# Another order and another spread over the engines for a chunk-selected attention with an ELU feed-forward block

## Chip, cores and metric

The kernel runs on one core of one Trainium2 chip. The metric is the device time of one execution in microseconds (us). The core has TensorE (PE, with its weight loads as PEld), VectorE (DVE), ScalarE (ACT), GpSimd (POOL) and SyncE (SP), and 16 DMA engines that are fed by queues. Each engine works off its own instructions in program order.

## The reference, cut to what matters

```python
batch, n_heads, seq, head_dim = (4, 8, 768, 64)      # q, k, v in float32
n_tokens, d_model, d_ff = (3072, 512, 2048)          # the block behind it
...
chunk = 32; nc = S // chunk; top_k = 6
k_min, k_max = k_chunks.min(axis=3), k_chunks.max(axis=3)
ub = sum(maximum(q * k_min, q * k_max), axis=-1)      # a bound for each query and chunk
ub = where(causal, ub, -1e9)
top_chunks = argsort(ub)[..., -top_k:]                # six chunks for each query
scores = where(sel & (pos_q >= pos_k), scale * q @ k.T, -1e9)
attn = softmax(scores) @ v
x = attn.transpose(0, 2, 1, 3).reshape(B * S, H * D)
h = x @ w_in
g = where(h > 0, h, exp(minimum(h, 0)) - 1)
out = g @ w_out
```

## The kernel before

Work is cut into eight units of 384 tokens. Units 0 and 1 are made of the first halves of batches 0 and 1, in quarters of 192 tokens: quarter `p` of both batches is unit 0, quarter `s` of both is unit 1. Units 2 to 7 are half a batch each: (batch 0, second half), (1, second half), (2, first), (2, second), (3, first), (3, second). Each unit has an attention part for four pairs of heads and then the feed-forward part (`mlp`).

The names of the entries, with batch, half or quarter, and pair in the digits:

- `ldk`, `ldq`, `ldv` load K, Q and V (on SP, five of the first K loads on ACT); `ldc` loads K once more in another layout for batches 2 and 3; `ec` copies constant rows into `lhs`. `w_in0` to `w_in2` and `w_out0` to `w_out3` load the weights on POOL's queue, converted on the way; the space of `w_out` serves as landing room for first loads of Q and V until then (`stage`).
- `kT` and `qT` transpose K and Q on PE (L409 for units 0 and 1, L549 later). `kmin`, `kmax` (L373, L492) and `ks` make the bounds of the chunks; `kt`, `ka`, `qt`, `qr`, `qa`, `qh`, `v`, `kb`, `ky`, `kv` are casts and copies (L326, L328, L339, L348, L350). `kd` is a transposing DMA.
- `ub` (L604) computes the bounds for the queries, and `ubT`, `max`, `lt`, `sT`, `mk` (L615 to L632, L328) turn them into mask rows.
- `sc` are score products (L696, L732, L786), `tr` the preset of a mask (L688), `ex` the exponentials (L704, L739, L801, L805), `tri` the triangular mask (L744, L818), `pv` the products with V (L758, L837), `rcp` and `on` the division (L648, L650). `px` and `xt`, or the transposing DMA `xd` (L661), turn the result into the feed-forward block's input.
- `h` is a product with w_in (L878, four matmuls, 16 entries to a unit), `e` its exponential (L885), `m` and `g` finish the activation (L887, L891), `o` are four matmuls with w_out (L902; L856 in the last tile, which is split into halves), `oe` copies the result out of PSUM and `out` stores it.
- `fill` is a small product of zeros that nobody reads (L941); there are 170 in the graph, and the list holds 40 of them.

A graph of operations is built first, each with its readers, writers and the engines that can do it. What runs is set by two strings: `ORDER` lists all operations, three characters for each (engine, then the operation's number in base 64), and `PLACES` gives, in order of first use, which buffer of its class each value takes. The program is emitted in the order of the list; every engine sees its own entries in that order, and waits come from the data and from the reuse of buffers:

```python
    for j in range(0, len(order), 3):
        o = g.ops[64 * DIGITS.index(order[j + 1]) + DIGITS.index(order[j + 2])]
        for b in o.bufs:
            if b.slot is None and b.cls != "fixed":
                b.slot = DIGITS.index(next(places))
        o.emit({"P": PE, "A": ACT, "D": DVE, "G": POOL, "S": SP}[order[j]])
```

So an engine may run ahead of the list where its own inputs are there, but never past an earlier entry of its own. The loads of W on POOL's queue stand behind POOL's arithmetic, and the loads on SP behind SP's other transfers.

Of the kernel before, what the change touches and what calls it, by code (L numbers as in the profile page):

```python
# [65 lines left out]
D8HSaCGbaAaRD8IA7ZPp0AaTA7-G8FSaxG8fApxGcWPpcD8JPp4GpyD8KA7+ApdPpoPpgPp8GpeDpfAppGpqD8LPpMAp1Ap9
DprSayGp2Dp3Ap5GpaDpzDpbD8MAphPpQScPApRAb6Gp6PpIGpiPpEDpjApNSoVDp7ApJPpUAb9Gb7Sf8PpYGpSDpTPpkApF
PqcSaUDpGG8NGpKDpLA8OGpODpPAplDpHGpmP8+SbCApZGp-ApVPq0A90P9rDpnGpWScKP8TSc+Dp+P97SbAG8tP96DpXAaB
SoUShlG8QPqdP8ZA98A8UG8sG99P91P93P8RP8XA9sA8-A92P9nA94Pq1P8VP9xP9lPq2A8YDaWP9wDaVA8SDbcA9mP9jP9t
DbDG95DbfP9bA8WP9aA9yG8PD9cP9pP9fA9uSbbA9kSaXShrA9oP9hP9PD9vA9gPq3A9qP9RDbvA9QD9dA9iG9zP9XP9WDbE  # L70
P9HP9AA9YGbyAq4A9IGbFGcUDcTGbqDbgP9BD9CPahGbiP9FP9TAaiA9GGbGA9UPkgD9DP9NDaYDaZPqeDbwDa+Da-A9SP9J
A9OPalPafAagPakP9LDb0A9MG9ZPa3G9VGajA9KPadPa7PqfAamP9+P9-Da0Aa8PabAa4DboSaEAacPa9Da1GanSb8S9eS9E
Pa5Pq6AaePb1Db4Db2Db5PaoSfgSq5Db3Sa2PkfAaaAa6AbxPapPbHGbhPq7GaDDaqPq8DarDbISasDbJDbKAaFAqgDbLAhw
Pq9Dd4DbMDdcDbNPqSPqqPqmAbdGbOPquSbeAqaDfiPqCAqTAbQGqUAhxGbPPcaAqnDqVGqoPbXDqpPbSPbYScNPc9AqrGqs
DqtDfhAqvAcXPqiPreShkAbZPr2AqDGfPAbTSg3Pr6Pq-ShyScYSqhAqjAddGbRGqwArfDqxPbUAcbSg4PqyGqEAr7DqFGcQ
SgaPcnPcoGqkDqlAq+GrgAbVGr8DrhDd8Dd0Ar3Gr4AcpPcyGr0Dr9Dr5AqzGqAPqKPcwAqLScVPqGPcBPcCGccAqHDr1DqM
DqBDbWSf5ProPqWAcDAcxAczPc6PqOPc4Ad7PciAqXDqNGqIDqJGb-Pc0GcEPb+GqYPckAc7DqZDc1AcjScRAclPriPraAc5
GcAPcFPcGPrjArbDcmGcqGdeSfjAqPDc2Dc8Ad1DcHAd5PcdPcrDrcDcIPcsDrdAd9GcODctDcuGd6GqQPcePruGcSDcfSgc
Ad3PdgDqRDhASf9PrpPrkScJPrlPrvDcgPrqDdiScvSc3DdhSchDdkSqbPrrPrIDdjSfWPs4SgbGd2PrwDdlAdbArsArJArm
As5DdmDdnPrMPdBPdISfVAdoShpPdtPrUGdqSrnAdCDfkDs6Pe6GrKSfYDrLPdrSf6ArVPe7GhuPrxGrWDs7PdJPrADflGda  # L80
AduAe8DrXDfmGfMArNPrEPrQPdFAryGrODrPPdvPsgAdKDfnDdLArBPs0GfOGrCArFArRDrGAdwPdzAdGGrSDrDSfXDrHAsh
PsoSg2DfLAdASg1PdDPrYGsiGdfAdsPdZDrTAspDsjGsqAdEDsrPswPdRSf4PeXPeWPdxGdHAs1Sf3Gs2De9DhCSfePs8AdS
Sg9SfQAdyDdpSfaArZDs3GfoPdMPdNGr-DgdPdTAeYSfxAsxShmPsAPe1Dr+GsyAd-DszGhtDfZDdOAdUPe3PssPexPelAs9
GsaAe2DdPAe4PscAstGsuPdXAemPdVDg0DsvGe5PewDsbPsBDfRPepPd+AdYAgeShnAdWPskPeaAsdDseAe0PebAfSSdQDsf
PeTAeyDecAslPeJPetDedPsMGffAeqAeKAeUPerPefPehSrzPfpSrtAeuAesAegPeRAeSPsNGezDfbPenAfUPejPeFGsmShv
DsnDfzGevPsOPeNGgfAeiAeoPeBDfySeeAekSf7PeLGhqDfqAeMAhFPeAPsGPePDg5DeVDeCPsHAeGGfTSfcDeDGf+AeQPeH
GeZPsIAeODf-SfuAeIPe+Pe-PsCPsJSeEDf0Df1PsPPsDDfvSf2GfJPs-PtKGfIGg8DfwAfsDfASfKDfBAfrPt2DfCPfDAfd
AsKAsEAs+AhzDftDfGPsSAg6SsLDfHAtLGggSfNGt0DfEGtMAt3DtNPsWGt4Pt6AsTAfFDt5Dt1PghGsUDsVDgiAsQPtiDgj
DgkAhsShBAt7AsXPtaDglGsYDsZAtjDgmDgnGtkAtbGtcPtGDtdPtqAtHGt8PtmDt9PtOGgoAtrAtnDtlAg7AgqPtePgsGto
PgyAgtDtpGtIDtJPgxPtyPgWDhKPgZGgpAgzAtfDgrGtsAgXPg-PguPtSPgGGtgDttPtCAg+PgUDthAtPPhcDhDAgHAgvPtu  # L90
Gh0PhbGtQSsRAgVDhODgADtRPgMAhPPtTAtvPgIPtYAtzGgwDhGDtwDtAPgLGgYGhMPtZAtDDtBDtxGhIPgBAgJPh6SsFPt-
DtEPh8DtFPgCAgNPh1Ph2AhdDgKDgOAhJPgQPu2PgPAh7Pt+Ah9GheDh3DgDDh4DhaPhfSh5Pu3PhgAhHAhLAu0PhSDgRPtU
PtVPu4DgESgFDhRDgSDhhSgTDhiShjPv4PucDhUPuwPu5AtWGhoAhNDhTAv5AudAhEGv6DhWDhVPuIDhXDhYGhZGueStXPuk
PijPibPiiDv7Au6Pi7PugAuJAuxDufPi1Gh-AicGuKAulAikGumPuoDuLAi8PifPiBAi2GuyDunPu8PuAAupPidGh+DuzAuh
Au9DuqDurPuQPi5AiCAuBGuaAieGuCSu1PuEPiDAigDubGuiDuDPi3PusDujAuRPuMDihAuFPveAiEGuGAi4Pi9DuHGuSAi6
PiFPuUAutAiaDuTAiGAuVPixPivGilPizPinAiyGuuDuvPimPuYPiJPiIDioAuNAiwAiKPiXDuOPvfPv0DuPAiYGi0PjxPj3
DhQGuWAuZPjwAiAGiHDipPitDuXDiLPj7Su7Av1Aj4Pj1PvgPj6Gv2Aj2AiuPirGu-Du+PjjPiNPiTDv3AisPiMAjkPi+Pjt
DiOAiUPv8Pv9Aj8AjyAjuPjfGjzDj5PiZPjrPiVAj0Dj9PiRDiPAi-AiWPjnPvhPjpAiSPjlPjaPjbAjsPvkAjmDviAjqDjv
PjhAjoPvlAjgPjADjcSiQAjiPjBPvaPvmDjdDjCSiqDjDPvbPvnSvjSjeSjEPvyPvqPvOPv-PvuPvGAvoAvPPvSAv+DvcPvC
GvQGw0DvRAvzAvvDw1PwaDvwDvxPw2AvrGvASvpAvTDvUAvDGvEDvBDvVPvKGvsAvHAwbGwcDvtAw3Pw6PvWPwiDwdPwmDvF  # L100
GvIAw7DvJPweGw8Gw4Dw5PwqAvXAvLPwwGvMGvYAwfDvNPwrPwCDw9AwnAwjDwgDvZPwsGwkDwoDwpDwlDwhPwDPwtPwEPwx
PwyPwzSvdAwuPwIPwJPwFSwvPwKPwLDwNDwMAwAAwGAwHAwOSwB
"""
PLACES = """
001002030450010621034005670061732032132110140412347026613607701373332320250060271703071135142022
503112123031600420024112017123230420536501174006220522064013062037373121713204331001207624254315
02116001146612712052890211761107ab02c0d563202740163e2002f240601306201054153373131506024146150002
31472201023431130530317520431061151240220g241210207310001060330121245114062204100152260301187707
a62112200bd509221c551414e67220246170314530674125620764117024640000657135100744122253102364145011
23140171035000450036205303116321033545611024002f206012712311125672300101240250067113221251280a14  # L110
370062101210b2d2310052091120c32e1766774320106743034234145267001322033270626107201143370151624375
220647055134240123625037022300011002074350002221g0136501527313413611610022757201a301402083421072
9f105320101122461221307162d50040156267230021020311b320251476c14430560130112110210677423061e30223
# [877 lines left out]
```

## Time and profile before

| | us |
|---|---|
| median of three runs (lowest, highest) | 280.38 (280.07, 280.51) |
| the profiled execution | 280.4 |
| its span, first to last instruction | 278.7 |
| granted TensorE clock, mean | 1.000 |

| engine | instructions | share of the span |
|---|---|---|
| PE | 2374 | 94% |
| DVE | 590 | 79% |
| ACT | 449 | 72% |
| POOL | 295 | 55% |

A profile page gives the busy time of each engine, the span in 40 slices, the DMA queues, the chain of work that ended last, and groups of instructions by line. In a row of a group stand line, engine, operation, output and input, count, then busy time and the mean length of one in ns, then the engine's idle time just before them and what ended it. A row of waits reads: engine, line and who was waited for, then us in total, times, and the longest. In a table of stretches each row has the stretch, its length and the busy time of each engine in it, then granted clock, DMA share and GB/s.

### The profile page before, as it was taken

How to read it: one execution, taken by the hardware profiler on the slowest of the kernel's cores; microseconds unless marked ns; L12 is line 12 of the kernel's file. 1: busy time of each engine (PE TensorE's matmuls, PEld its weight loads, DVE VectorE, ACT ScalarE, POOL GpSimd, SP SyncE). 2: the span in 40 equal slices, each digit the busy share in tenths (PEclk: the TensorE clock that was granted, in tenths of full speed). 3: DMA queues.
4: the chain of work that ended last, by engine and by line, in shares of the span. 5: the costliest groups of instructions: out<-in, count | busy, mean ns of one | idle time of the engine just before them, and what ended most of it. 6: DMA issues, size and time to landing. Idle time of an engine off the chain costs nothing.

```text
span 278.7 us, 6784 instructions
## 1 busy us (share of the span) xinstructions
PE 260.7 (94%) x2374; PEld 160.8 (58%) x2404; DVE 220.8 (79%) x590; ACT 202.0 (72%) x449; POOL 153.3 (55%) x295
## 2 busy tenths in 40 slices
PE   0798999999999999999999999999999999999995
PEld 0576655585556755565566456665565456665653
DVE  1489998489999999999999997997898766632850
ACT  2066977578898997999599369995898289872621
POOL 6187578212886657878189437763476077300610
PEclk9999999999999999999999999999999999999999
DMA  8999999969959649997499388993900230032002
GB/s 155 214 203 216 212 207 222 202 139 199 199 129 206 146 87 243 210 194 122 121 214 205 69 189 160 184 199 93 224 3 2 58 115 0 2 80 92 1 9 106
DMA packets 118690, 39.25 MB, mean 141 GB/s; under 512 B 111104, under 2 KB 113408, under 8 KB 118656
## 3 DMA queue, kind: packets, MB, share of 16 engines
q1 hardware_dynamic: 112928, 33.67, 59.3%
q0 software_dynamic: 2672, 4.19, 8.2%
q10 hardware_dynamic: 3056, 0.95, 1.7%
q8 instruction: 19, 0.31, 0.5%
q14 instruction: 15, 0.12, 0.2%
HBM read 30.41 MB, written 6.29 MB: 132 GB/s over the span
## 4 chain that ended last, share of the span: by engine, by line
PE 64%; DVE 11%; DMA 10%; issue 5%; ACT 4%; POOL 4%; SPq 1%; DVEq 0%; POOLq 0%; ACTq 0%
PE bank L902 23%; PE bank L878 18%; PE bank L786 8%; PE bank L837 5%; DMA w_in<-in_moe_w_in_dram 5%; DMA f<-in_k_dram 3%; DVE gT L891 3%; POOL m L887 2%; PE bank L409 2%; DMA xt<-on 2%; DVE km L492 2%; PE bank L604 2%; ACT e L885 2%; DVE kst L373 2%; PE bank L758 1%
## 5 line engine op out<-in xcount | busy, mean ns | idle before, releaser
L878 PE MATMUL bank<-xt,w_in 128*128 128x384 bf16 x512 | 92.3, 326 | 0.8 <-DMA w_in<-in_moe_w_in_dram 0.3
L902 PE MATMUL bank<-w_out_sb,gT 128*128 128x512 bf16 x339 | 86.5, 379 | 2.6 <-DVE gT L891 0.7
L887 POOL TENSOR_SCALAR m<-e 128x384 f32<-128x384 f32 x104 | 54.3, 530 | 56.9 <-ACT e L885 51.9
L891 DVE SCALAR_TENSOR_TENSOR gT<-bank,m 128x384 bf16<-128x384 f32 x128 | 66.1, 549 | 15.0 <-POOL m L887 13.5
L801 ACT ACTIVATE pt<-bank 128x384 bf16<-128x384 f32 (+1 forms) x144 | 67.6, 554 | 5.2 <-PE bank L786 4.2
L878 PEld LDWEIGHTS <-w_in 128*128 128x128 bf16 x512 | 49.1, 98 | 34.3 <-issue 2.4
L885 ACT ACTIVATE e<-bank 128x384 f32<-128x384 f32 x128 | 59.4, 496 | 12.3 <-PE bank L878 8.9
L902 PEld LDWEIGHTS <-gT 128*128 128x128 bf16 x368 | 34.3, 97 | 35.2 <-issue 2.5
L786 PE MATMUL bank<-rhs,lhs 96*128 96x384 bf16 (+2 forms) x240 | 44.6, 293 | 0.1
L818 POOL TENSOR_TENSOR pt<-pt,tri 128x256 bf16<-128x256 bf16 (+1 forms) x30 | 26.5, 894 | 10.6 <-ACT pt L801 5.6
L326 ACT ACTIVATE o<-bank 128x512 f32<-128x512 f32 (+1 forms) x18 | 10.6, 590 | 29.5 <-PE bank L902 26.3
L786 PEld LDWEIGHTS <-lhs 96*128 96x128 bf16 x240 | 22.1, 97 | 15.1 <-issue 0.6
L492 DVE TENSOR_REDUCE km<-kc 96x64 f32<-96x1024 f32 x16 | 30.5, 1923 | 0.0
L837 PEld LDWEIGHTS <-pt 128*128 128x128 bf16 x576 | 21.0, 97 | 4.3 <-issue 0.6
L373 DVE TENSOR_REDUCE kst<-bank 128x12 f32<-128x384 f32 x32 | 16.4, 545 | 7.8 <-PE bank L409 7.8
L837 PE MATMUL bank<-vext,pt 128*128 128x65 bf16 x576 | 22.2, 193 | 0.3 <-DVE gT L891 0.3
L328 POOL COPY rhs<-selT 32x384 bf16<-32x384 bf16 (+1 forms) x19 | 12.8, 673 | 14.3 <-DVE selT L632 13.4
L650 DVE TENSOR_TENSOR on<-bank,rcp 128x384 bf16<-128x384 f32 (+1 forms) x40 | 19.7, 495 | 0.6
L328 POOL CAST rhs<-qt 64x384 bf16<-64x384 f32 x33 | 17.5, 540 | 3.1 <-ACT qt L326 1.4
L648 DVE RECIPROCAL rcp<-bank 128x6 f32<-128x6 f32 (+1 forms) x40 | 7.1, 182 | 11.4 <-PE bank L837 7.1
L805 ACT ACTIVATE pt<-bank 128x512 bf16<-128x512 f32 x24 | 14.6, 617 | 0.9 <-PE bank L786 0.8
L328 DVE COPY o<-bank 128x512 f32<-128x512 f32 (+1 forms) x8 | 4.6, 584 | 12.7 <-PE bank L856 6.7
(104 smaller groups left out, 314.0 us busy)
## 6 DMA issues: line engine op xcount, KB each, us to landing
out_dram<-o SPq DMA_DIRECT2D x21, 256.0 KB, 2.4
f<-in_v_dram SPq DMA_DIRECT2D x20, 256.0 KB, 4.4
f<-in_k_dram SPq DMA_DIRECT2D x18, 256.0 KB, 4.7
fx<-in_q_dram SPq DMA_DIRECT2D x32, 96.0 KB, 3.2
kc<-in_k_dram SPq DMA_DIRECT2D x8, 384.0 KB, 4.9
w_out_sb<-in_moe_w_out_dram POOLq DMA_DIRECT2D x4, 512.0 KB, 11.4
f<-in_q_dram SPq DMA_DIRECT2D x6, 256.0 KB, 11.6
w_in<-in_moe_w_in_dram POOLq DMA_DIRECT2D x2, 512.0 KB, 8.6
```

Of the source, the lines that this page charges most:

```text
L328: eng[e].tensor_copy(out=dst, in_=src)
L373: g.op(("kmin", "kmax")[w] + tag, (DVE,), lambda e, w=w, op=op: nc.vector.tensor_reduce(out=cs(w), in_=src(), axis=AX.X, op=op), reads=[(b ...
L492: nc.vector.tensor_reduce(out=ap(km)[0:96, y, w], in_=ap(kc)[0:96].rearrange("p (w d) -> p d w", d=D), axis=AX.X, op=op), reads=[(kc, 0)], ...
L786: nc.tensor.matmul(ap(banks[hd])[:, o + pc:o + pc + wd], lhsT=apl(ls, G)[0:96, pr, hd, P * kb:P * (kb + 1)], rhs=ap(rs)[0:96, hd, c0 - HS ...
L801: lambda e, hd=hd, pt=pt, banks=banks, wtot=wtot: nc.scalar.activation(out=ap(pt)[:, hd, PAD:PAD + wtot], in_=ap(banks[hd])[:, 0:wtot], fu ...
L818: eng[e].tensor_tensor(out=view, in0=view, in1=tri[:, 64:64 + P].rearrange("p (a b w) -> p a b w", a=1, b=1) .to_broadcast([P, 2, len(dg), ...
L837: nc.tensor.matmul(view()[:, hd, qi, :], lhsT=ap(pt)[:, hd, P * qi + off:P * qi + off + P], rhs=ap(vx[b])[:, kb, 2 * r + hd, :], start=(kb ...
L878: nc.tensor.matmul(ap(bank)[:, 0:HS], lhsT=w_in_sb[x][:, kk, c0:c0 + 2 * P - 1:2], rhs=ap(xT[i, kk]), start=(kk == 0), stop=(kk == NKK - 1))
L885: g.op(f"e{i}.{fc}", (ACT,), lambda e, eb=eb, bank=bank: nc.scalar.activation(out=ap(eb), in_=ap(bank)[:, 0:HS], func=AF.Exp), reads=[(ban ...
L887: g.op(f"m{i}.{fc}", (POOL, DVE), lambda e, eb=eb, mb=mb: eng[e].tensor_scalar(out=ap(mb), in0=ap(eb), scalar1=-1.0, scalar2=1.0, op0=AOT. ...
L891: nc.vector.scalar_tensor_tensor(out=ap(gt), in0=ap(bank)[:, 0:HS], scalar=0.0, in1=ap(mb), op0=AOT.max, op1=AOT.min),
L902: nc.tensor.matmul(ap(bank), lhsT=ap(gts[fc])[:, P * tt:P * (tt + 1)], rhs=w_out_sb[:, fc, :], start=(fc == 0), stop=(fc == NFC - 1))
```

## The change

Only the two strings `ORDER` and `PLACES` are replaced; no function is touched. Both lists hold the same 1969 operations, each once, the 40 fills among them. 188 operations change their engine. By engine the entries go: PE 620 to 620, ACT 455 to 458, DVE 454 to 449, POOL 266 to 267, SP 174 to 175. The kinds that change most: `m` DVE 24 to 34 and POOL 104 to 94; `tri` DVE 22 to 18 and POOL 34 to 38; `ks` DVE 4 to 0 and POOL 12 to 16; `kb` ACT 4 to 2, DVE 3 to 0, POOL 5 to 10; `kt` ACT 11 to 14, DVE 5 to 2.

```diff
 ORDER = """
-S0YA0VS0rS0xS0XS2fS0vA0tS2iA0uS0wA0sS0yD0iS2gA0WD00G06D03D09G0bG04S0zPjGG0jG0cD0kG0lG0aP0MD0OG08
...
+A0WS0wS2gS0xA0uA0sS0YS0VS0vS0XA0rG0hD03D09A0tD06G0aS2fG0cG0iG04G0lG0jS0zA05S2iG0bS0yS0BS0+P0DP11
...
 """
 PLACES = """
-001002030450010621034005670061732032132110140412347026613607701373332320250060271703071135142022
...
+001023040500000123450006102117510504551552503610347714212340212072531072003003012430152162122102
...
 """
```

The first places of the two lists, decoded (engine letter and entry; A is ACT, S is SP, G is POOL, D is DVE, P is PE):

```
before: S ldq1p10, A ldk1p00, S ldk0p00, S ldq0p10, S ldq1p00, S ldk0s00, S ldq0p00, A ldk0p10, S ldq0s10,
        A ldk0p11, S ldq0p01, A ldk0p01, S ldq0p11, D kz, S ldk0s10, A ldk1p10, D zeros, ...
        P fill, ... P kT0p1, D kmax0p1, ... P kT1p0, ... P qT1p1, P kT0p0
after:  A ldk1p10, S ldq0p01, S ldk0s10, S ldq0p10, A ldk0p11, A ldk0p01, S ldq1p10, S ldk1p00, S ldq0p00,
        S ldq1p00, A ldk0p00, G kq, D idz, D tnz, A ldk0p10, ... S ldk0s00, ...
        P kT0p0, P kT1p0, P kT0p1, P kT1p1, P qT0p0, P qT1p1
```

Places of some entries on the list, counted from 0:

| entry | before | after |
|---|---|---|
| ldv0p0, ldv0p1, ldv1p1, ldv1p0 (V of unit 0) | 22, 36, 65, 81 | 23, 28, 29, 42 |
| ldq1s10 | 82 | 135 |
| w_in0, w_in1, w_in2 | 103, 152, 197 | 92, 141, 150 |
| w_out0, w_out1, w_out2, w_out3 | 201, 204, 293, 295 | 189, 238, 323, 331 |
| fills before the first h | 24 | 27 |
| first h (entry) | 219 (h0.1) | 217 (h0.0) |
| ex0s30, tri0s3 | 340, 382 | 308, 326 |
| first o (entry) | 325 (o0.2.0) | 311 (o0.0.0) |
| first use of w_out3 | 379 (o0.2.3) | 381 (o0.2.3) |
| ub20, the selection of batch 2 | 1041 | 1045 |
| first h of unit 7 | 1876 (h7.2) | 1875 (h7.6) |

In the last places, the final quarter of the last tile (`out7.2.1`) is stored by SP instead of ACT, and the half before it (`oe7.2.0`) is copied by DVE instead of ACT.

More of the change, by code (lines that the diff above doesn't have):

```diff
@@ new lines @@
+P1pP1vD2qA2sP1oA1wA1xD10P1qS2PD0-PjJD2DPjWG0SA1rP1OP2JP1HPjLP1DP1ID0RP2wA2KP1SP1NPjNG2uD1PA1sD1Q
+P1yP1RD2NA2xA2FP25P26S2RA2yP1EA2AG0PP1YGmkG2rPjYG2EG14D1TA2GP1XP1zGmlPjPA2LPjRD27D1UG2zP1AD1FP1V
+P3gD1ZD1GP33D1-D1JA1BS2vS2mPj-S2IS2VS3fS2TS4-D0eD1KPjTP29PjVG08P1+D28P1LG2tD1WA1CP20P2aGmmA3hPjX
+PjZP2XD21D22D1gG2HPj+D2YP3lP23D2bPk1D2cP38A1MP2dD24A2+Pk0D3mPk2D2ZPk4D3nA2ePmqA3cD3iPk6D3oPk8Pk3
+PmyPmuPkaD3pPmGD3qA3dPk5PmOD3rG30Pk7AmrPk9GmnG1dG0fGmsPkcA34A35S4+PkbD3aDmtD39G3sP3JG2-PmKAmzDmA
+PmSA36A3tG3bDmBP3wAmHGmIAmPA3KDmQA2MG3vDmRAmvPkeAmLD3yDmJA31P4FPmCP3HA4GG37P41P4DS50S4XGmwGmMG3j
@@ L120 @@
+90307202310c401214053062142331330422012012302110120331043201621701f412002506271380612000g1021114
+10201012035e17513202206459151a002420350102d1434141370b103221360742010207410131056020321054130022
+671c3610280010223537f11g44051142220260130721157201202250a34631521421504396021106220141e251053725
+070761b7102301560123740567230017232230106247103120d62021110050a14c21f010701651832120913240102460
+1e20g1002677011
 """
```

139 lines of the change are left out of this document (64 added, 75 removed).

## The prediction

> **What bounds the kernel now.** I read the page's busy times first, then stages of my own cutting in the table of stretches, then the waits of PE, then the chain of waits, and last single instructions of the first 55 us.
>
> ```profile
> span 278.7 us, 6784 instructions
> PE 260.7 (94%) x2374; PEld 160.8 (58%) x2404; DVE 220.8 (79%) x590; ACT 202.0 (72%) x449; POOL 153.3 (55%) x295
> core 0: us, PE busy (x) PEld busy (x) DVE busy (x) ACT busy (x) POOL busy (x), PEclk, DMA share, GB/s
> 8.30:16.00 7.70, 7.02 (x35) 5.68 (x36) 5.40 (x12) 0.99 (x3) 2.88 (x7) 1.00 1.39 203
> 16.00:30.10 14.10, 12.63 (x188) 9.13 (x188) 12.44 (x40) 10.50 (x22) 11.34 (x40) 1.00 1.29 216
> 30.10:44.40 14.30, 13.43 (x118) 8.31 (x116) 13.24 (x55) 11.32 (x25) 9.70 (x18) 1.00 1.15 215
> 44.40:60.00 15.60, 15.44 (x160) 10.29 (x163) 10.17 (x27) 10.38 (x22) 6.33 (x10) 1.00 0.93 190
> 60.00:133.50 73.50, 71.88 (x703) 44.74 (x708) 70.18 (x176) 67.66 (x156) 49.80 (x87) 1.00 0.83 174
> 133.50:254.30 120.80, 118.95 (x1054) 70.11 (x1071) 98.03 (x259) 90.25 (x203) 62.72 (x107) 1.00 0.52 109
> 254.30:278.70 24.40, 20.96 (x128) 12.41 (x127) 10.20 (x23) 9.34 (x20) 6.08 (x12) 1.00 0.15 55
> ```
>
> TensorE is busy for 260.7 of 278.7 us. Both orders hold the same 620 entries of PE, the 40 fills among them, so PE's work is the same and the span can change only by PE's idle 18.0 us, or where PE is busy with fills that only pass the time. From 44.4 to 254.3 us the table leaves 0.16 + 1.62 + 1.85 = 3.6 us of idle PE; after 254.3 it leaves 3.4. The rest, 11.0 us, lies before 44.4, most of it before the first transposition. There DVE is nearly full (12.44 of 14.10, 13.24 of 14.30), and the DMA share column stays above 1.1.
>
> ```profile
> PE bank L758 <- POOL vext L339: 0.7, 1, 0.7
> 0.82 4.07 DMA f<-in_k_dram
> 4.91 5.05 DMA f<-in_k_dram
> 8.39 1.03 PE L409 MATMUL bank<-ident_f,f 96*128 96x96 f32 x5 [6.32 <-DMA f<-in_k_dram]
> 9.30 0.56 DVE L373 TENSOR_REDUCE kst<-bank 128x12 f32<-128x384 f32 x1 [6.83 <-PE bank L409]
> 28.55 0.41 DVE L650 TENSOR_TENSOR on<-bank,rcp 128x256 bf16<-128x256 f32 x1
> 30.10 2.19 PE L878 MATMUL bank<-xt,w_in 128*128 128x384 bf16 x12
> 44.40 2.75 PE L902 MATMUL bank<-w_out_sb,gT 128*128 128x512 bf16 x11 [0.44 <-DVE gT L891]
> 9.30:29.00 19.70, 17.64 (x204) 13.03 (x204) 17.00 (x47) 10.45 (x22) 13.27 (x44) 1.00 1.33 211
> 29.00:44.40 15.40, 14.53 (x138) 9.32 (x131) 14.08 (x57) 12.36 (x28) 10.66 (x21) 1.00 1.15 214
> ```
>
> So the start has three marks: the first transposition of K (8.39), the first product with w_in (30.10), the first with w_out (44.40). Between them DVE works off one series, 17.00 us in 19.70 and 14.08 in 15.40. From 44.4 on PE is dense. A shorter start is therefore kept as long as nothing later is short of cover.
>
> **The start, first mark.** In the new order the first transposition is kT0p0, which needs the last two of the five K loads on ACT's queue; before it was kT0p1, which needed the third and fourth.
>
> ```profile
> q1 hardware_dynamic: 4162, 1.04, 61.6%
> q10 hardware_dynamic: 2768, 0.69, 39.9%
> f<-in_k_dram ACTq DMA_DIRECT2D x2, 192.0 KB, 4.6
> f<-in_k_dram ACTq DMA_DIRECT2D x3, 96.0 KB, 4.9
> ```
>
> In the first 10 us (queue rows of that window) ACT's queue (q10) took about 40% of what moved. Its five loads held 2 x 192 + 3 x 96 = 672 KB, the last landing at 4.91 + 5.05 = 9.96. The new five hold 192 + 4 x 96 = 576 KB. The transfers began near 2.2 us (an estimate from the same rows), so the last now lands at 2.2 + 576/672 x 7.8 = 8.9; I take 9.1, bounds 8.4 (today's start) and 10.0 (today's fifth load). Today PE has a pause before 10.01; the new order has six transpositions ready in a row, all their loads by my count of bytes on SP's queue being in by 10. DVE's first reduction follows at 9.1 + 0.9 = 10.0 instead of 9.30: **+0.7 us**.
>
> **The start, second mark.** From that reduction to the last `on` before the first h there were 47 DVE entries, busy 17.00 us, done at 28.96.
>
> ```profile
> L328 DVE CAST kt<-bank 128x384 bf16<-128x384 f32 x5 | 2.6, 543 | 0.1
> L350 DVE TENSOR_SCALAR qr<-qt 128x384 f32<-128x384 f32 x3 | 1.7, 580 | 0.5 <-ACT qt L326 0.5
> L373 DVE TENSOR_REDUCE kst<-bank 128x12 f32<-128x384 f32 x32 | 16.4, 545 | 7.8 <-PE bank L409 7.8
> L328 DVE COPY lhs<-kt 64x384 bf16<-64x384 bf16 x4 | 1.2, 311 | 0.1
> ```
>
> The new order has 44 there, priced by busy time over count: ten leave (three kt at 0.52, a qr 0.57, a kmax 0.51, two ka at 0.30; a v, a ks and `warm`, together an estimated 0.8: 4.0 us), seven come (two ka 0.6; a v, a qa and three fills, an estimated 1.8: 2.4 us). The series is 1.6 us shorter. With the idle 2.7 us it has today it ends at 10.0 + 15.4 + 2.7 = 28.1, and the first h starts, as today, 1.14 later, at 29.2: **-0.9 us**, the later start included. V sooner takes away PE's 0.7 us wait on vext, which lies inside that idle time; late next is the s-unit's q of batch 1, 53 places further back on the list, but by bytes it lands near 22 and is used near 25. On SP only loads and one copy of constants stand ahead of it, none with a wait of note.
>
> ```profile
> L409 PEld LDWEIGHTS bank<-ident_f,f x4: 230/230/230, 15.1 to 15.6; 96*128 96x128 f32 x4
> L409 PEld LDWEIGHTS bank<-ident_f,f x4: 140/140/143, 16.7 to 17.0; 96*128 96x128 f32 x4
> ```
>
> These rows show PE slower by 230/140 until about 16 us, though the clock column says 1.00: 6.0 us after the pause that ended at 10.01. With no pause after 9.1 the same 6.0 us end at 15.1, and PE does 0.9 x (1 - 140/230) = 0.35 us more work by then. As DVE sets the pace, and PE holds 27 fills before the first h (24 today), I take nothing for it. [...]
>
> **The start, third mark.** From the first h to the first o DVE had 32 entries after the first ubT; the new list has 26 (eleven leave and five come, 2.0 us by their rows; a g, an m, a lt and a max now come behind the first o, two mk go to other engines). By DVE the first o would come at 41.9. By PE: the listed PE work from first h to first o is 12.3 us before and 11.6 after, by the rows of its kinds; 13.43 x 11.6/12.3 = 12.7, so 41.9 without stalls, 42.8 with today's 0.9. The same amount of PE work was done at 44.0 today. Gain so far 1.2 to 2.1; I take 1.6, that is **-0.7 us** on top. The work put off is covered from 44.4 to 60, where DVE is idle for 5.4 us and ACT for 5.2; without that cover its 2.0 us would come back.
>
> **W_out.** All loads but the W ones run on SP; the W ones wait in POOL's list.
>
> ```profile
> 24.59 13.48 DMA w_in<-in_moe_w_in_dram
> 40.06 0.72 POOL L301 DMA_DIRECT2D w_out_sb<-in_moe_w_out_dram  x1
> w_out_sb<-in_moe_w_out_dram POOLq DMA_DIRECT2D x1, 512.0 KB, 10.2
> DMA to landing us min/median/max: 8.0/11.4/14.6
> 53.81 1.03 PE L902 MATMUL bank<-w_out_sb,gT 128*128 128x512 bf16 x4
> ```
>
> W_in's last half is issued earlier (three POOL entries are no longer ahead) and used 1.9 us of PE work later, so its 0.3 us wait goes. But the last quarter of W_out, issued at 40.06 and landed at 50.3 for a use at 53.8, now stands behind tri0s3, which waits for ex0s30 on ACT. Walking ACT's 20 entries from the first `e` (30.1) to ex0s30 at about 0.52 each, with 0.7 of waiting for the first selection, gives 41.2; the tri (0.95) ends at 42.2, and the load lands after 8.0 to 10.2, at 50.2 to 53.1. Its use, 1.6 sooner, would be at 51.7. Cost 0 to 1.4, the mean of the landings puts it at the use; I take **+0.4 us**.
>
> **The middle.** 188 of the 1969 entries change engine.
>
> ```profile
> L887 POOL TENSOR_SCALAR m<-e 128x384 f32<-128x384 f32 x104 | 54.3, 530 | 56.9 <-ACT e L885 51.9 <-DVE gT L891 1.6 <-DVE kt L328 0.7
> L887 DVE TENSOR_SCALAR m<-e 128x384 f32<-128x384 f32 x24 | 12.0, 503 | 1.0 <-ACT e L885 0.7
> L326 ACT ACTIVATE lhs<-kt 64x384 bf16<-64x384 bf16 x15 | 7.8, 519 | 0.3
> ```
>
> Over the whole run ten `m` go from POOL to DVE (+5.0 us there), and tri, ks, kt, kb and small ones leave DVE (some -6.8): DVE about -1.8 us, ACT +2.2, POOL +1.1, off the bound in sum. By stage it is less even: between the first o and the selection of batch 2 (today 44.4 to 133.5) ACT gets 180 entries for 173, 7 x 0.52 = 3.6 us, POOL 12 more, DVE 3 more. ACT's idle time there is 5.2 + 5.84 us, so the cover holds, thinly. Bounds -0.7 (half of PE's 1.62 idle goes) to +3.6; I take **+0.2 us**, nearer to the first, because PE's idle 1.62 us there is small beside DVE's 95% and ACT's 92%.
>
> **The end.** The last products are split as before. The last quarter of a tile is issued on SP instead of as ACT's second; both issues wait for the same DVE copies. I take 0, bounds -0.3 and +1.8 (SP's 128 KB output stores took 3.5 us, ACT's 1.7).
>
> ```profile
> out_dram<-o SPq DMA_DIRECT2D x4, 128.0 KB, 3.5
> out_dram<-o ACTq DMA_DIRECT2D x2, 128.0 KB, 1.7
> ```
>
> **Sum.** -0.9 - 0.7 + 0.4 + 0.2 = -1.0 us. The profiled execution took 280.4 (span 278.7 and 1.7 around it), the median of the three runs is 280.38, so the two stand level: **279.4 us**.
>
> **Rivals.** A change of 0.2% (0.56 us) is about what a measurement of this kernel can tell from none.
>
> First, *the gain is swallowed by W_out*: the last quarter lands at 53.1 and the kernel goes on from there as today, when this use was at 53.3 for the same PE work; 280.2. For it: the DMA share stays over 1.1 to 45 us whatever the order. Against: fewer loads compete by then.
>
> Second, *the middle gets slower*: ACT, 92% busy from 60 to 133.5 (67.66 of 73.5), rises to about 97%, and its queue hands exponentials late to PE's sums. With half of the 3.6 us on the path: 279.4 + 1.8 = 281.2; all of it gives 283.0. It decides from where ACT's idle time in this stretch falls under some 3 us. For it: DVE is 95% busy beside it. Against: PE lost only 1.62 us there today.
>
> Third, *W_out's last quarter is issued only at its place on the list*, 3.3 us of PE work behind the first o, that is at 42.2 + 3.3 = 45.5: it lands at 55.7, 2.4 later than the same PE work was reached today, 282.8. It decides from an issue later than 43.1. Against: a queue of POOL runs ahead of the list when its own inputs are there.
>
> Fourth, *PE paces the start* and the faster rate comes earlier: 279.4 - 0.35 = 279.05. [...]
>
> That the change does nothing can't be: the list is what is emitted.
>
> **How the numbers follow.** Forecast 0.38, swallowed 0.14, slower middle 0.26, late issue 0.14, PE pacing 0.08. Faster: 0.38 + 0.08 = 0.46; same 0.14; slower 0.40. The low end takes the third mark at its full 2.1 (0.5 more), W_out without a wait (0.4), and the middle at -0.7 (0.9 below the sum's +0.2): 279.4 - 1.8 = 277.6. The high end lies 1.0 above the slower middle, at 282.2; only the late issue and the worst of the middle are outside. The forecast's own range is 278.4 to 279.8.
>
> **What would show it.** First transposition at 8.9 to 10.0; first h near 29.2; first o near 42.2; issue of W_out's last quarter near 42.5 and a PE wait of at most 1.4 us on it; PE's idle time from 60 to 133.5 within 1 us of 1.62; last product 1.0 us earlier. Wrong, if the first o is not before 43.5, or if the stretch behind it loses more than 1 us.

## The result, and the profile after

The changed kernel took 277.9 us (median; 277.3 to 278.57) where the kernel before took 280.44 (280.07 to 281.03) on the same chip: a ratio of 0.9908, 95% interval 0.9879 to 0.9938, or 2.5 us less. The two profiled executions, 277.3 and 280.4, differ by 3.1. The forecast of 279.4 had the sign, but the time lies 1.5 below it, outside the forecast's own range (278.4 to 279.8) and near the low end of the whole one.

First the page after, and the stretches between the same marks as before: first transposition, first h, first o, 60 us, selection of batch 2 (`ub20`), first h of the last unit, end.

```profile
span 275.6 us, 6820 instructions
PE 259.8 (94%) x2404; PEld 159.8 (58%) x2404; DVE 219.1 (80%) x585; ACT 202.0 (73%) x453; POOL 153.2 (56%) x296
core 0: us, PE busy (x) PEld busy (x) DVE busy (x) ACT busy (x) POOL busy (x), PEclk, DMA share, GB/s
8.27:30.24 21.97, 19.00 (x227) 14.63 (x228) 17.06 (x47) 12.00 (x27) 11.63 (x45) 1.00 1.31 212
30.24:42.04 11.80, 11.80 (x115) 7.81 (x112) 10.97 (x51) 10.74 (x24) 7.81 (x17) 1.00 1.14 206
42.04:60.00 17.96, 17.96 (x201) 12.28 (x200) 14.35 (x43) 14.72 (x31) 7.15 (x13) 1.00 0.88 184
60.00:131.03 71.03, 69.91 (x670) 42.68 (x667) 65.72 (x160) 63.70 (x150) 53.82 (x95) 1.00 0.90 184
131.03:251.26 120.23, 120.20 (x1072) 69.98 (x1071) 98.28 (x258) 90.21 (x203) 63.37 (x107) 1.00 0.50 105
251.26:275.60 24.34, 20.96 (x129) 12.43 (x127) 12.03 (x28) 9.09 (x19) 4.15 (x8) 1.00 0.21 76
```

From the first h to 60 us TensorE has no idle time at all. The gain is not ahead of the first h and not at the end, which still takes 24.34 us where it took 24.35. One caution: the page before counts 2374 matmuls and this one 2404, for the same work, so TensorE's busy time before is a little too low and its idle time too high. The marks do not suffer from that. They are the starts of TensorE's own rows:

| mark | before | after | difference | change in the stretch |
|---|---|---|---|---|
| first h | 30.10 | 30.24 | +0.1 | |
| first o | 44.40 | 42.04 | -2.4 (-2.0 at equal PE work) | -2.1 |
| selection of batch 0's second half (`ub01`) | 67.70 | 65.76 | -1.9 | 0 at equal PE work |
| selection of batch 1's second half (`ub11`) | 103.26 | 100.36 | -2.9 | -1.0 |
| selection of batch 2 (`ub20`) | 133.45 | 131.03 | -2.4 | +0.5 |
| first h of the last unit | 254.35 | 251.26 | -3.1 | -0.7 |
| last instruction | 278.7 | 275.6 | -3.1 | 0 |

"At equal PE work" sets the first o beside the time at which the kernel before had done the same amount of TensorE's work (44.0 us, from the prediction).

The rows that answer to the prediction's single ones follow view by view. The chain of waits and the timeline of TensorE, at the start:

```profile
4.25 5.09 DMA f<-in_k_dram
```
```profile
8.27 0.39 PE L409 MATMUL bank<-ident_f,f 96*128 96x96 f32 x1 [8.27 <-DMA f<-in_k_dram]
9.39 2.66 PE L409 MATMUL bank<-ident_f,f 96*128 96x96 f32 x15 [0.73 <-DMA f<-in_k_dram]
30.24 0.81 PE L878 MATMUL bank<-xt,w_in 128*128 128x384 bf16 x4
42.04 1.03 PE L902 MATMUL bank<-w_out_sb,gT 128*128 128x512 bf16 x4
```

The last K load of ACT's queue ends at 9.34 and the run of transpositions starts at 9.39; the first h comes at 30.24, the first o at 42.04. The weight loads of the transpositions (shortest, median and longest ns, then first and last start):

```profile
L409 PEld LDWEIGHTS bank<-ident_f,f x19: 169/230/230, 9.4 to 13.4; 96*128 96x128 f32 x19
L409 PEld LDWEIGHTS bank<-ident_f,f x6: 139/144/230, 13.3 to 15.9; 96*128 96x128 f32 x6
```

They stay at 230 ns until 13.4 and are at 144 behind that. VectorE's series between the marks, in the timeline of VectorE and POOL, and as a stretch:

```profile
10.24 0.56 DVE L373 TENSOR_REDUCE kst<-bank 128x12 f32<-128x384 f32 x1 [8.61 <-PE bank L409]
16.06 0.95 POOL L252 MEMSET pt<- 128x1024 bf16 x1
16.22 1.09 DVE L328 COPY lhs<-kt 64x384 bf16<-64x384 bf16 x1
23.04 0.18 DVE L648 RECIPROCAL rcp<-bank 128x4 f32<-128x4 f32 x1 [1.53 <-ACT pt L704]
```
```profile
10.24:29.57 19.33, 17.09 (x215) 12.98 (x214) 16.39 (x45) 11.84 (x26) 11.06 (x43) 1.00 1.30 212
```

The series starts at 10.24 and needs 19.33 us, 16.39 of them busy. Among these is one copy of 1.09 us, of a kind that took 0.31 on average before, beside a memset of POOL. Last W_out, in POOL's timeline and in the DMA issues (KB each, us to landing):

```profile
41.75 0.91 POOL L744 TENSOR_TENSOR pt<-pt,tri 128x384 bf16<-128x384 bf16 x1 [1.64 <-ACT pt L739]
42.61 0.76 POOL L301 DMA_DIRECT2D w_out_sb<-in_moe_w_out_dram  x1
```
```profile
w_out_sb<-in_moe_w_out_dram POOLq DMA_DIRECT2D x1, 512.0 KB, 8.0
```

The last quarter is issued at 42.61 and lands 8.0 us later, at 50.6; TensorE has no wait on it.

### The profile page after: what moved, and what is told of

The parts are those of the page before. It is cut to its first block, busy times and chain, and to the rows that moved or that the text cites. A ratio compares the mean times of both kernels' runs of the same rounds, so it can differ in the third digit from the quotient of the medians.

```text
span 275.6 us, 6820 instructions
## 1 busy us (share of the span) xinstructions
PE 259.8 (94%) x2404; PEld 159.8 (58%) x2404; DVE 219.1 (80%) x585; ACT 202.0 (73%) x453; POOL 153.2 (56%) x296
## 3 DMA queue, kind: packets, MB, share of 16 engines
HBM read 30.41 MB, written 6.29 MB: 133 GB/s over the span
## 4 chain that ended last, share of the span: by engine, by line
PE 84%; DVE 9%; DMA 4%; issue 1%; ACT 1%; POOL 0%; DVEq 0%; ACTq 0%; POOLq 0%
PE bank L878 28%; PE bank L902 27%; PE bank L786 10%; PE bank L837 5%; PE bank L604 3%; DMA f<-in_k_dram 3%; PE bank L409 2%; DVE kst L373 2%; PE bank L549 2%; PE bank L758 1%; DVE km L492 1%; PE bank L732 1%; PE bank L856 1%; DMA xt<-on 1%; PE bank L941 1%; DVE on L650 1%
## 5 line engine op out<-in xcount | busy, mean ns | idle before, releaser
L878 PE MATMUL bank<-xt,w_in 128*128 128x384 bf16 x512 | 92.0, 326 | 0.2
L902 PE MATMUL bank<-w_out_sb,gT 128*128 128x512 bf16 x368 | 90.2, 379 | 0.2 <-DVE gT L891 0.2
L887 POOL TENSOR_SCALAR m<-e 128x384 f32<-128x384 f32 x94 | 49.3, 533 | 49.5 <-ACT e L885 41.2
L878 PEld LDWEIGHTS <-w_in 128*128 128x128 bf16 x512 | 49.5, 98 | 34.0 <-issue 2.3
L902 PEld LDWEIGHTS <-gT 128*128 128x128 bf16 x368 | 34.4, 97 | 34.3 <-issue 1.5
L818 POOL TENSOR_TENSOR pt<-pt,tri 128x256 bf16<-128x256 bf16 (+1 forms) x35 | 31.7, 912 | 13.8 <-ACT pt L801 7.0
L326 ACT ACTIVATE o<-bank 128x512 f32<-128x512 f32 x19 | 11.4, 598 | 18.1 <-PE bank L902 18.1
L328 POOL COPY rhs<-selT 32x768 bf16<-32x768 bf16 (+1 forms) x17 | 11.6, 683 | 12.0 <-DVE selT L632 11.2
L887 DVE TENSOR_SCALAR m<-e 128x384 f32<-128x384 f32 x34 | 15.2, 452 | 2.1 <-ACT e L885 1.9
```

Of the source, the lines that this page charges most:

```text
L328: eng[e].tensor_copy(out=dst, in_=src)
L818: eng[e].tensor_tensor(out=view, in0=view, in1=tri[:, 64:64 + P].rearrange("p (a b w) -> p a b w", a=1, b=1) .to_broadcast([P, 2, len(dg), ...
L878: nc.tensor.matmul(ap(bank)[:, 0:HS], lhsT=w_in_sb[x][:, kk, c0:c0 + 2 * P - 1:2], rhs=ap(xT[i, kk]), start=(kk == 0), stop=(kk == NKK - 1))
L887: g.op(f"m{i}.{fc}", (POOL, DVE), lambda e, eb=eb, mb=mb: eng[e].tensor_scalar(out=ap(mb), in0=ap(eb), scalar1=-1.0, scalar2=1.0, op0=AOT. ...
L902: nc.tensor.matmul(ap(bank), lhsT=ap(gts[fc])[:, P * tt:P * (tt + 1)], rhs=w_out_sb[:, fc, :], start=(fc == 0), stop=(fc == NFC - 1))
```

## The experiments

Two questions: is it the order or the engines, and which part of the list carries the 2.5 us? The theory was that the start (the stretch up to the first o) carries it. The rival theories were that the engines of the middle carry it, that TensorE's early slow phase does, or that V's earlier loads do. Ratios below are to the kernel before on the same chip, with 95% intervals. "Entry" is a place on the list.

**Order alone, engines alone.** Each list entry keeps its old engine under the new order, or gets its new engine under the old order:

```diff
 # e1: new order
-(engine_after[op], op) for op in after
+(engine_before[op], op) for op in after
 # e2: old order
-(engine_before[op], op) for op in before
+(engine_after[op], op) for op in before
```

> The new order and the new places, but each of the 188 entries on the engine that it had before. If the gain comes from the order of the start (what stands ahead of the first product with w_out), most of it stays: 278.0 to 279.3 against 280.4. If it comes from the spread over the engines, nothing stays or the time gets longer, 280.4 or more. If order and engines only work together, the time is above 281, because entries now stand on engines for which the order was not made.

> The order before, with the 188 entries on their new engines. If the order of the start carries the gain: 280.4 to 282, no gain. If the spread over the engines carries it: 278 to 279.

Measured: 296.58 us, ratio 1.0549 (1.0528 to 1.0570), and 301.39 us, 1.0713 (1.0682 to 1.0744). Neither half of the change is worth anything by itself; both make the kernel slower. An engine's queue is part of the order: with an entry on another engine, what stands behind it on that queue starts at another time, as e5 shows further down on SyncE's queue (a load issued at 99.36 us behind three other entries, at 96.42 without them). So "order" and "engines" cannot be priced apart, and the cuts that follow are made along the list instead.

**New head, old rest, and the reverse.** The first 450 entries (to about 62 us) from one list, what is left from the other:

```diff
-order = after
+order = after[:450] + [x for x in before if x not in after[:450]]   # e3
+order = before[:450] + [x for x in after if x not in before[:450]]  # e4
```

> The new list (order, engines, places) for its first 450 entries, about 62 us, then all that is left in the old order; a few buffers change place at the seam. By the marks of the two traces (the second selection of batch 0 starts at 65.76 against 67.70) the start brings 2.0 us: 278.4, 277.9 to 279.0. If the gain of the start is lost again because the old rest isn't made for it: 280 or more. If the gain lies behind 62 us: 280.4.

> The old list for its first 450 entries, then all that is left in the new order. If the start brings 2.0 us of about 3.1 in the profiled executions, the rest brings 0.5 to 1.1: 279.3 to 279.9. If the gain lies in the rest: 278. If the old start is not made for the new rest: above 280.4.

Measured: the new head alone 0.9946 (0.9925 to 0.9967), so 1.5 us of the 2.5; the new rest alone 1.0011 (0.9992 to 1.0031), no gain. The stretches show why the head keeps only part. These are the ones from `ub01` to `ub11` in the kernel before and in the one with the new head:

```profile
67.70:103.26 35.56, 34.81 (x329) 21.54 (x332) 33.96 (x82) 32.49 (x75) 24.42 (x42) 1.00 0.74 158
66.28:102.81 36.53, 35.42 (x331) 21.43 (x330) 34.63 (x82) 32.35 (x74) 23.45 (x42) 1.00 0.79 169
```

With the new head it takes 36.53 us where it took 35.56 before and 34.60 after. The lead of 1.4 us at `ub01` (66.28 against 67.70) shrinks to 0.45 at `ub11` (102.81 against 103.26). The old order of this stretch, entered earlier, gives two thirds of that lead back. Nor does e4 show that the rest is worth nothing: its cut cost 1.1 to 1.4 us ahead of `ub01` (38.88 us from the first h, where the old order takes 37.43 to 37.81 in four traces), and its stretch to `ub11` then took 34.31, as in the new order.

**New to 103 us.** The same cut at entry 760.

```diff
+order = after[:760] + [x for x in before if x not in after[:760]]   # e5
```

> The new list for its first 760 entries (to about 100 us), the rest in the old order. By the marks of the traces the stretch from the second selection of batch 0 to that of batch 1 costs 35.56 us in the old order and 34.60 in the new. If the start and this stretch carry the gain together: 277.7 to 278.6, that is 0.9 to 1.6 below the kernel with only the new head (279.5). If the head's gain was lost to the seam alone and the stretch has no part in it: 279.5 again.

Measured: 1.0015 (0.9993 to 1.0037). That contradicted the head's gain, until its timelines, of TensorE and then of SyncE, showed this:

```profile
102.31 0.97 PE L878 MATMUL bank<-xt,w_in 128*128 128x384 bf16 x5 [2.53 <-DMA xt<-on]
```
```profile
95.12 1.60 SPq L310 DMA_DIRECT2D lhs<-econst  x1
98.24 0.40 SPq L310 DMA_DIRECT2D f<-in_v_dram  x1
98.68 0.58 SPq L310 DMA_DIRECT2D out_dram<-o  x1
99.36 1.25 SPq L661 DMA_TRANSPOSE xt<-on  x1
```

The cut put the last transposing load of unit 2's rows behind three old entries of SyncE's queue, one of them held until 98.24. The load was issued at 99.36, against 96.42 after, and TensorE waited 2.53 us for it.

**The cut mended, and moved.** One entry moved ahead of the three; then cuts at entry 828, which leave this load wholly in the head.

```diff
 # e9, on top of e5: behind entry 760
-ec111, ldv200, out1.2.0, ..., xd013
+xd013, ec111, ldv200, out1.2.0, ...
+order = after[:828] + [x for x in before if x not in after[:828]]   # e10
+order = before[:828] + [x for x in after if x not in before[:828]]  # e11
```

> New order and engines for the first 760 entries, then the old ones, as in e5_new_to_103; one entry is moved: the last transposing load of unit 2's rows (xd013) stands ahead of the three SyncE entries (ec111, ldv200, out1.2.0) behind which e5 had it. Theory (the new head gains as far as it goes, and e5 lost that gain to its seam's queue): TensorE's wait of 2.5 us at 102.3 goes, the half of unit 1 that starts at 103.29 in e5 starts at 100.4 to 101, and the ratio is 0.990 to 0.994 in place of 1.0015. Rival (e5's loss was in the work at the seam and not in the queue): 1.000 to 1.002, with another wait of some 2.5 us at the same place.

> New order and engines for the first 828 entries (all of unit 2's transposing loads and the start of unit 1's second half are among them), then the old ones. Theory (start to first o, -2.0 us in the traces, and the stretch from 62 to 103 us, -1.0, carry all of the gain, and the rest is worth nothing either way): ratio 0.990 to 0.993, unit 2's first chunk at 131 to 131.7 (133.45 old, 131.03 new). Rival (the rest of the new order brings its own part, or a head pays only with the rest that was found for it): 0.995 to 1.000.

> The complement: old order and engines for the first 828 entries, then the new ones. Theory: the rest is worth nothing, so 0.999 to 1.002, and from 133 us on its marks follow those of before within 0.5 us. Rival (the new rest has a gain of its own, from 0.2 us, which the marks from unit 1's second half to unit 7's first h differ by in the traces, to 1 us): 0.996 to 0.999.

Measured: 0.9990 (0.9972 to 1.0009), 1.0015 (0.9992 to 1.0039) and 1.0093 (1.0058 to 1.0129). The theory misses all three times. The rival of e9, another wait of some 2.5 us near the same place, came about much as it was put (the range it gave overlaps the measured interval); the rivals of e10 and e11 did not. Up to the cut the theory holds: the wait of 2.5 us is gone in e9, and `ub11` starts at 100.54 (e9) and 100.34 (e10), as in the new order (100.36) and unlike e5 (103.29). But behind its cut each of the three has a new wait of about the same size, in their TensorE timelines, e9, e10, e11 in this order:

```profile
105.43 10.29 PE L878 MATMUL bank<-xt,w_in 128*128 128x384 bf16 x52 [2.61 <-DVE ubT L615]
```
```profile
111.18 2.76 PE L878 MATMUL bank<-xt,w_in 128*128 128x384 bf16 x16 [2.71 <-DVE gT L891]
```
```profile
112.95 2.76 PE L878 MATMUL bank<-xt,w_in 128*128 128x384 bf16 x16 [2.44 <-DVE gT L891]
```

In e10 the timeline of ACT, VectorE and POOL shows what the wait is made of: in turn they wait for each other over the gate of the feed-forward block (`e` on ACT, `m` on POOL, `g` on VectorE). That each brings a queue from two lists to it is the likely reason, which no run tested.

```profile
108.17 0.97 ACT L885 ACTIVATE e<-bank 128x384 f32<-128x384 f32 x2 [1.14 <-POOL m L887]
108.17 0.56 DVE L891 SCALAR_TENSOR_TENSOR gT<-bank,m 128x384 bf16<-128x384 f32 x1 [1.90 <-POOL m L887]
110.02 1.47 POOL L887 TENSOR_SCALAR m<-e 128x384 f32<-128x384 f32 x3 [1.40 <-DVE gT L891]
110.56 0.56 DVE L891 SCALAR_TENSOR_TENSOR gT<-bank,m 128x384 bf16<-128x384 f32 x1 [0.70 <-POOL m L887]
```

So each of the four cuts near 103 to 109 us brought a wait of 2.4 to 2.7 us of its own, in either direction, and the times of e5, e9, e10 and e11 price the cuts, not the parts. What they leave standing are the marks away from the cut. Put side by side over all traces that hold one order through a stretch, away from a cut, the marks price the parts better than the times do:

| stretch | new order, us | old order, us |
|---|---|---|
| first h to `ub01` | 35.52 (after, e5, e6, e8, e9, e10) | 37.43 to 37.81 (before, e7, e11, e12) |
| `ub01` to `ub11` | 34.30 to 34.60 (after, e6, e8, e9, e10) | 35.08 to 35.56 (before, e7, e11, e12) |
| `ub11` to `ub20` | 30.67 to 30.71 (after, e4, e6, e8) | 30.18 to 30.41 (before, e3, e7, e12) |
| `ub20` to the first h of the last unit | 120.23 to 120.97 (after, e4, e6, e8, e11) | 120.77 to 121.17 (before, e3, e5, e7, e9, e12), 122.41 (e10) |

The first stretch gains about 2.0 us, the second 0.5 to 1.3, and the third loses 0.3 to 0.5, each without overlap; in the last the two orders overlap, so a gain there is not shown.

**New up to the first h only.** The first 214 entries.

```diff
+order = after[:214] + [x for x in before if x not in after[:214]]   # e12
```

> New order and engines for the first 214 entries, which end just ahead of unit 0's first h, then the old ones. Theory (the gain up to the first o lies in the order of the work between first h and first o, since the first h itself comes at 30.24 new and 30.10 old): first h at 30.2 to 30.8, first o at 44.0 to 44.9 as in the old order, ratio 0.999 to 1.002. Rival (the gain is made at the start, by what DVE and the queues have done or loaded by the first h, V sooner among it, and only shows behind it): first o at 42 to 42.9 and a ratio of 0.993 to 0.996.

Measured: 280.57 us, ratio 0.9971 (0.9951 to 0.9991), between the ranges of the two theories, so the ratio does not decide; the profiled span is 278.9, against 278.7 before. The marks decide: first h at 30.41, first o at 44.65, as in the old order. With the new start, the old order of the work behind it makes the old time. The two kernels hold the same matmuls from the first h to `ub01`, but for two fills, so these stretches, e12's first and the changed kernel's second, price the order of that work directly:

```profile
30.41:67.96 37.55, 36.39 (x354) 23.86 (x352) 30.83 (x103) 27.99 (x62) 19.30 (x37) 1.00 1.03 200
```
```profile
30.24:65.76 35.52, 35.52 (x357) 23.79 (x354) 30.77 (x105) 30.30 (x66) 17.92 (x37) 1.00 1.01 198
```

It is 2.03 us: 1.16 of TensorE's idle time (36.39 busy of 37.55, then 35.52 of 35.52) and 0.87 of busy time. The idle time is three waits of e12 on results of ACT and VectorE, all up to the first o, as its timeline of TensorE shows:

```profile
31.39 3.57 PE L878 MATMUL bank<-xt,w_in 128*128 128x384 bf16 x21 [0.33 <-ACT xt L326]
38.17 0.82 PE L878 MATMUL bank<-xt,w_in 128*128 128x384 bf16 x4 [0.19 <-ACT e L885]
44.65 2.75 PE L902 MATMUL bank<-w_out_sb,gT 128*128 128x512 bf16 x12 [0.64 <-DVE gT L891]
```

The busy part is for the most part waiting too. In these profiles a short wait can disappear under a matmul that counts as busy on: from 36.10 to 37.50 us TensorE of the kernel before is busy for 1.40 of 1.40 us, while its weight loads stop twice, for 0.16 and 0.37. They stop in the selection products of L604, for `qr` and for `gT` (e12 has the same rows of these matmuls, 0.19 to 0.20 us later), while in the changed kernel the first 16 of these products run in one go:

```profile
36.40 0.14 PEld L604 LDWEIGHTS bank<-qt,kst 64*32 64x32 f32 x2 [0.16 <-DVE qr L350]
36.91 0.15 PEld L604 LDWEIGHTS bank<-qt,kst 64*32 64x32 f32 x11 [0.37 <-DVE gT L891]
```
```profile
36.09 0.56 PE L604 MATMUL bank<-qt,kst 64*32 64x192 f32 x16
```

Counted from the start of each matmul to that of the next, without idle time, the 32 products of L604 take 1.38 us in e12 and 0.81 after, which is 0.57 of the 0.87; the 48 of L732, some of which stand right ahead of a wait, take 3.82 and 3.56; the 48 of L902 are level (10.36 and 10.37). So nearly all of the 2.0 us are waits of TensorE for VectorE and ACT between the first h and the first o, which the new order does not have. VectorE's busy time up to `ub01` is the same (30.83 and 30.77); ACT has 2.3 us more. Which moved entries took the waits away was not tested one by one.

**V late.** The changed kernel with three of unit 0's four loads of V back at their old places on the list.

```diff
-ldv0p1 at 28, ldv1p1 at 29, ldv1p0 at 42
+ldv0p1 at 36, ldv1p1 at 65, ldv1p0 at 81
```

> The new order, but three of the four V loads of unit 0 stand on the list where they stood before (36, 65 and 81 instead of 28, 29 and 42). If V sooner carries a part of the gain: PE waits for V's casts again (0.7 us before) and the time is 278.4 to 279.5. If it lies beside DVE's series, as the prediction held: 277.7 to 278.2.

Measured: 277.96 us, ratio 0.9876 (0.9851 to 0.9902), level with the changed kernel's 277.9 on another chip. TensorE does not wait for V in its trace. Its first h is at 31.07 instead of 30.24, its last unit's first h at 252.58 instead of 251.26, and still its median is that of the changed kernel: its profiled execution is the slowest of six, and the five other traces with the new start and no added fills have their first h anywhere from 30.38 to 30.77. V's earlier load carries no part that these runs can tell.

**TensorE warm from the start.** 30 more fills at the head of each list, so that the weight loads are quick when K arrives:

```diff
+D zeros, P fill x30          # e6 on the changed kernel, e7 on the one before
 ...
 P kT0p0                      # e7: P kT0p1
```

> The new order with 30 more fills in front of the first transposition, in time in which PE waits for the first K, and the zeros set first. If TensorE's slow phase (weight loads of 230 ns to 13.4 us) costs time: it ends before the first transposition and the time falls by 0.3 to 1.5 us, to 276.4 to 277.6. If DVE sets the pace of the start, as the prediction held: 277.9, within 0.3. If the fills delay the first transposition: 278.2 to 279.

> The old order with the same 30 fills in front. The slow phase lasted to 16.0 us there, 2.5 longer than in the new order. If that is what the new order gains at the start: 279 to 279.8, and more than the new order gains from the same fills. If DVE sets the pace: 280.5 to 281.

Measured: 278.09 us, 0.9876 (0.9852 to 0.9901), and 281.18 us, 1.0000 (0.9977 to 1.0023). The fills did what they were put there for, as TensorE's timeline of e6 shows: its 15 transpositions took 1.46 us instead of 2.66. But the granted clock then fell to half, as a stretch of e6 shows (the clock is the third number from the end), where both kernels without the added fills have 1.00 from 8 to 20 us.

```profile
1.75 4.46 PE L942 MATMUL bank<-zeros 128*128 128x256 bf16 x27
9.57 1.46 PE L410 MATMUL bank<-ident_f,f 96*128 96x96 f32 x15 [0.82 <-DMA f<-in_k_dram]
```
```profile
12.40:17.90 5.50, 5.50 (x32) 3.85 (x32) 4.50 (x10) 3.15 (x8) 1.89 (x10) 0.50 1.32 195
```

So e6 had a slow stretch too, only a later one (its weight loads of L410 have a median of 230 ns from 12.3 to 16.7 us), and the test is weaker than intended. In e6 the first h hardly followed TensorE's rate: it came at 30.06, 0.18 earlier, with 15 transpositions 1.2 us quicker and 5.5 us at half clock. VectorE's series sets that mark there. In e7 it did move, the wrong way: to 31.65, 1.55 later than before. TensorE waited 1.80 us for a cast of V on POOL, where it waited 0.72 before, and behind that wait its clock was lower once more (a mean of 0.58 in the second row, after 0.70 from 12 to 16 us and 1.00 from 16 to 24):

```profile
22.98 0.37 PE L759 MATMUL bank<-vext,pt 128*128 128x65 bf16 x7 [1.80 <-POOL vext L340]
24.00:28.00 4.00, 3.88 (x46) 3.51 (x41) 2.93 (x13) 2.02 (x4) 2.60 (x6) 0.58 1.19 201
```

In neither order did the early fills make the kernel quicker.

## Why the prediction was right in sign and short in size

**The start, first mark: right for the run of transpositions.** First transpositions at 8.27 (a single one) and 9.39 (the run of them), against 9.1 with bounds 8.4 and 10.0; VectorE's first reduction at 10.24 against 10.0.

**The start, second mark: wrong, by 1.0 us.** The step that failed is "the series is 1.6 us shorter". VectorE's busy time was to fall from 17.00 to 15.4 and came to 16.39. Most of that is the copy of 1.09 us, 0.8 more than its price; the rest, some 0.2, is the other prices. Its idle time stayed (19.33 - 16.39 = 2.94, where 2.7 was assumed), but is another one: 1.53 us waiting for an exponential of ACT. The series ended at 29.57 instead of 28.1, and the first h followed 0.67 behind it instead of 1.14. Adding up entries priced a series by its content, and the contents met other neighbours. The 0.9 us expected here did not come: the first h moved by +0.1, and it lies at 30.24 to 30.77 in the six traces with the new start, at 30.10 to 30.39 in the three with the old one (before, e4, e11).

**The clock.** The prediction's own reading was that the slow weight loads would last the same 6.0 us, to 15.1. They did not: they took 230 ns until 13.4, 4.0 us behind the start of the run at 9.39, and 144 behind that. Why the slow rate lasted 6.0 us in the one kernel and 4.0 in the other is not shown. The price put on it, nothing, was right all the same: the quicker rate came sooner than predicted and the first h did not move.

**The start, third mark: right in place, mis-sized.** First o 42.04 against 42.2. From the first h it was to take 13.0 us and took 11.80, so 2.0 to 2.1 us are gained there instead of 0.7. The step that failed is the scaling: the listed work of 11.6 us was raised to 12.7 by the old busy time over the old list (13.43 over 12.3). The stretch took 11.80 without idle time, so the list was nearly right by itself, and of the 1.1 us by which the old busy time exceeds its list some 0.6 was waiting at L604 that counts as busy (1.38 us from start to start before, as in e12, and 0.81 after). For the same reason the premise that the span can change only by PE's 18.0 us of idle time was too narrow. The two errors, 1.0 too much ahead of the first h and 1.4 too little behind it, nearly cancel by luck: 1.6 predicted at equal work, 2.0 measured.

**W_out: +0.4 was 0.** Its chain was right (tri until 42.66, issue at 42.61, 8.0 us to land at 50.6), and the landing is near the earlier of the two bounds (50.2), and TensorE did not wait for it. The rivals of a swallowed gain and of a late issue fall with it.

**The middle: +0.2 was -0.4 up to `ub20`, with a sign that changes inside.** From the first o's lead of 2.0 the kernel goes to 2.9 at `ub11` and 2.4 at `ub20`. The first part, whose old order has 0.75 us of idle TensorE between `ub01` and `ub11`, gains 1.0:

```profile
65.76:100.36 34.60, 34.48 (x332) 21.36 (x331) 30.67 (x77) 30.71 (x73) 25.51 (x45) 1.00 0.87 177
60.00:133.50 73.50, 72.38 (x709) 43.95 (x707) 67.90 (x174) 65.22 (x153) 54.57 (x96) 1.00 0.88 180
```

Idle time from 60 to 133.5 is 1.12, within the 1 us of 1.62 that the prediction named. ACT is 89% busy there (65.22 of 73.5) and not the 97% of the rival with the slower middle: the work put on ACT was done sooner, where there was room: from the first o to 60 us it is 82% busy (14.72 of 17.96) where it was 67% (10.38 of 15.60). From `ub20` to the last unit another 0.7 us came in these two traces, for which the prediction had no term; over the other traces the two orders overlap in that stretch, so it may be the spread of executions.

**The end: right**, 0.

In sum: the median's 2.5 us are about 2.0 made between the first h and the first o, and some 0.5 behind it (1.1 in the two profiled executions), where 0.5 to 1.3 are gained up to `ub11` and 0.3 to 0.5 given back up to `ub20`. The first is shown by e12 and by the same stretch in ten traces, the rest by the marks of eight or nine. The sign was right for the reason given, a shorter stretch ahead of the first o, but no term of the sum had its size: -0.9, -0.7, +0.4 and +0.2 were +0.1, -2.1, 0 and -0.4. The low end of the range rested on a full third mark, no wait on W_out and a gain in the middle, and that is close to what came.

## What to carry to other kernels

Price a reordering by the stretch in which its bounding engine waits, and do not take its busy time for work: here some 0.8 of 2.0 us of waiting hid under running matmuls, and gaps in the weight loads showed it. A sum of entries on a neighbouring engine put the first h 1.0 us too early, and the first o came out right by luck. Two whole lists cannot be priced by grafting one on the other: every cut at 103 to 109 us brought a wait of 2.4 to 2.7 us, so read such experiments by the marks away from the cut, and look for a new wait just behind it before believing the time. And one transposing load behind the wrong entries of a DMA queue made TensorE wait 2.53 us, as long as the whole change gained; what it costs in the end is not shown, since in e9 another wait took its place.

## What the runs showed of the hardware

In e9 and e7 the granted clock was lower after a pause of TensorE. In e9 the wait of 2.61 us ended at 105.43; from 106.5 to 109.7 the weight loads of L878 start 0.32 us apart, where 27 of them take 4.34 behind that (0.16 each), as their timeline shows, the mean clock is 0.58 from 106 to 108 and 0.57 from 108 to 110, and the whole stretch has 0.95:

```profile
106.49 0.15 PEld L878 LDWEIGHTS <-w_in 128*128 128x128 bf16 x1 [0.15 <-issue]
106.81 0.15 PEld L878 LDWEIGHTS <-w_in 128*128 128x128 bf16 x1 [0.17 <-issue]
109.69 4.34 PEld L878 LDWEIGHTS <-w_in 128*128 128x128 bf16 x27 [0.17 <-issue]
```
```profile
100.54:135.06 34.52, 31.30 (x297) 18.26 (x296) 29.28 (x75) 28.81 (x68) 24.17 (x41) 0.95 0.81 174
```

That is some 11 products at half rate, about 1.7 us on top of the wait (an estimate from these rows). In e7 a wait of 1.80 us that ended at 22.98 was followed by a mean clock of 0.58 from 24 to 28 us; in e10, with a wait of 2.71, and in e11, with one of 2.44, the stretch around the wait has 1.00 (100.34 to 133.26 and 103.03 to 135.94). Over e9's executions the same split appears: the mean granted clock was 0.998 or more in five of twelve, which took 280.5 to 280.8 us, and 0.992 to 0.994 in the other seven, which took 281.5 to 282.2. In e9 the kernel thus lost more than the wait's own length. What brought the lower clock, and why e10 and e11 kept theirs, is not shown.

Second, the granted-clock column read 1.00 over 8 to 13 us in both kernels while the weight loads of L409 took a median of 230 ns, where like ones later took 140 (before, from 16.7 us on) and 144 (after, from 13.3 us on). So here the length of like instructions showed a slow stretch that the column did not.

Third, VectorE's copy of 1.09 us (16.22 to 17.31) beside POOL's memset of 0.95 (16.06 to 17.01). A copy of the same kind and shape took 0.26 in the same trace, at a time when POOL ran nothing (27.02 to 29.66):

```profile
28.30 0.26 DVE L328 COPY lhs<-kt 64x384 bf16<-64x384 bf16 x1
```

The long one ended 0.30 us behind the memset, about what the short one took in all. That the memset held it up is not shown: no run moved the memset away from this copy.
